# Output order by eight copies of token lists, and a third buffer for gathered rows, in a fused attention and expert kernel

## The chip, the cores and the metric

The kernel runs on one core of one Trainium2 chip. The metric is the device time of one execution in microseconds (us), the median of several runs. PE is TensorE, DVE is VectorE, ACT is ScalarE, POOL is GpSimd, and SP is SyncE, which issues most DMAs.

## What is computed

Attention with a band mask (4 batches, 8 heads, 576 positions, 64 per head) gives 2304 tokens of 512 numbers. Each token goes to one of 8 experts, and what comes out goes through a last layer with a cosine.

```python
def _moe_ref(x, expert_emb, tau, w1, w2):
    logits = xn @ en.T / tau            # xn, en: x and expert_emb at length 1
    expert_idx = np.argmax(logits, axis=1)
    probs = softmax(logits)
    gate_w = probs[np.arange(N), expert_idx]
    for e in range(E):
        mask = expert_idx == e
        h = np.maximum(x[mask] @ w1[e], 0.0)
        out[mask] = gate_w[mask, None] * (h @ w2[e])

def _moe2_ref(x, w_in, w_out):
    h = x @ w_in
    g = h * np.cos(h)
    return g @ w_out
```

## The kernel before

**Stage 1 (to about 147 us): attention and routing.** 18 tiles of 128 tokens. A tile's result goes to DRAM as rows of `x_d`. For each token the kernel finds the expert and the rank among that expert's tokens. `scatter` (L590) then writes each token's pair (token number, gate) by an indirect DMA into `tok_r`, which has a region of REG = 2688 pairs for each expert, zeroed at the start. So region e begins with the list of expert e's tokens, and zeros follow. `counts` (L701) makes `off`, the number of tokens before each expert, and its integer copy `meta`.

**Stage 2 (to about 435 us): the experts, one after another.** For expert e the job `list` loads 384 pairs of its region into `ix`, on SP (L854). For each of three blocks c of 128 tokens: `rows` gathers 128 rows of `x_d` into a tile `xr` by an indirect DMA on POOL (L859); `gate` multiplies them by the gates on DVE (L863); `turn` transposes them on PE (L868); `x hi` and `x lo` split them in two halves of 16 bits on ACT (L873) and DVE (L875), in the tile `xT`. The products follow: `mm` of even number (L1002) makes h, `relu` and `relu_lo` (L957, L961) split it, `mm` of odd number (L971) makes y. The third block has products of its own (`tail`, L979), which run only for an expert with more than 256 tokens. `emit_Y` (L944) puts y into `yT`, with expert e's columns from `off[e]` on, so `yT` holds the tokens sorted by expert. Beside this, expert weights are loaded (L241, 1 MB each, five buffers), measured (L250) and split (L273 on ACT, L275 on DVE), and the weights of the last layer are fetched (L766), rebuilt from 64-bit words (L772 to L784) and split (L806, L808).

**Stage 3: the last layer** in five blocks of columns of `yT` (u at L1186 and L1200, o at L1224). The rows that come out are in sorted order, so an indirect DMA writes each tile of 128 rows to its tokens' places in `out` (L1292), by the list `idx`.

**Where `idx` comes from.** `places` (L918) works out on DVE, in four operations, each token's place in the sorted order, `pu`. `place` (L928) then writes 128 token numbers to these places in `tok_d` by an indirect DMA on POOL, 18 times. `placed` (L936) loads `tok_d` into `idx` on SP.

**What sets the order.** In stage 2 the jobs are given to a planner (`Plan`, L77) with a queue, a cost and the jobs that they come after. It emits them by its own estimate of start times, and where several could start within a small time of each other it takes the one with the longest way to the end (`rank`). So every engine, and SP's queue of DMAs, has one fixed order, and a job that is not ready holds up what stands behind it. The buffers enter as jobs to come after: `rows` number k comes after `turn` number k - 2, for two `xr` buffers (L1040):

```python
plan.add(("rows", e, c), "POOL", 1.1, lambda e=e, c=c: x_do(e, c, "rows"), ("list", e), ("turn", (k - 2) // 3, (k - 2) % 3), ("rows", (k - 1) // 3, (k - 1) % 3))
```

Of the kernel before, what the change touches and what calls it, by code (L numbers as in the profile page):

```python
# [19 lines left out]
ALU = mybir.AluOpType  # L20
AX = mybir.AxisListType
ENG = mybir.EngineType
# [33 lines left out]
CUT = 4  # L56

BIAS1 = {'lo': -5, 'scale': -5, 'k': -5, 'v': 6, 'sent': -8, 'counts': -5, 'load': -10}
BIAS = {'u first': 15, 'csquare': 5, 'off': -3, 't lo': 22, 'g': 5, 'yb lo': -2, 'places': -5}
HOLD1 = 0.6  # L60
HOLD = 0.35
TAIL = 1.3
# [103 lines left out]
def tile_kernel(ctx, tc, qh, kh, vh, c16_h, c32_h, emb, tau, w1h, w2h, win_h, wout_h, out):  # L166
# [5 lines left out]
    x_d = dram.tile([NTOK, D], F32, name="x_d")  # L172

    tok_r = dram.tile([E * REG, 2], U32, name="tok_r")
    tok_d = dram.tile([NTOK, 1], U32, name="tok_d")

    c32 = const.tile([128, 256 + E + NT], F32, name="c32")
    ident, perm, iota, tokf = c32[:, 0:128], c32[:, 128:256], c32[:, 256:256 + E], c32[:, 256 + E:256 + E + NT]
# [12 lines left out]
    tri = const.tile([128, E, E], F32, name="tri")  # L191
    off = const.tile([128, E], F32, name="off")
    meta = const.tile([1, 2 * E + 1], I32, name="meta")

# [33 lines left out]
    with tc.manual_schedule():  # L228
        wst = ctx.enter_context(tc.tile_pool(name="wst", bufs=5, side="left"))
        with ExitStack() as p12:  # L230
            c12 = p12.enter_context(tc.tile_pool(name="c12", bufs=1, side="left"))
            zero = c12.tile([128, 512], U16, name="zero")
            wtp = p12.enter_context(tc.tile_pool(name="wtp", bufs=4, side="left"))
            wsm = p12.enter_context(tc.tile_pool(name="wsm", bufs=3, side="left"))
            stg, wt = {}, {}
# [70 lines left out]
            with ExitStack() as p1:  # L306
# [16 lines left out]
                head = lambda j: slice(64 * j, 64 * j + 64)  # L323
                blank = cst.tile([128, E * REG // 64], U32, name="blank")
                tau_b = cst.tile([128, 1], F32, name="tau_b")
                ent = cst.tile([128, 4, E], F32, name="ent")
                q_t = {}

# [428 lines left out]
            class Conv:  # L757
# [28 lines left out]
                def flat(self, g):  # L786
                    return self.pieces[g].rearrange("p a n -> p (a n)")
# [46 lines left out]
            with ExitStack() as p2:  # L834
# [20 lines left out]
                    return ix  # L855

                def x_rows(ix, c):
                    xr = hs.tile([128, D], F32, name="xr", tag="xr")
                    G.indirect_dma_start(out=xr, out_offset=None, in_=x_d, in_offset=bass.IndirectOffsetOnAxis(ap=ix[:, c, 0:1], axis=0))  # L859
                    return xr  # L860

# [36 lines left out]
                why = "numbers of tokens"  # L898
                zb = zero.bitcast(BF16)
                for t in (*h3, y3) + (y3,) * WARM2:  # L900
                    T.matmul(out=t.rearrange("p a b -> p (a b)"), lhsT=zb[:, 0:128], rhs=zb[:, 0:512], start=True, stop=True)
                nre = [nc.values_load(wide[0:1, e:e + 1], engines=[ENG.PE], min_val=0, max_val=len(TAILS), skip_runtime_bounds_check_because=why) for e in range(E)]
                T.matmul(out=y3.rearrange("p a b -> p (a b)"), lhsT=zb[:, 0:128], rhs=zb[:, 0:512], start=True, stop=True)
                offr = {}

                def offset(e, q):
                    engine = {"DVE": ENG.DVE, "ACT": ENG.Activation}[q]
                    offr[e, q] = nc.values_load(meta[0:1, e:e + 1], engines=[engine], min_val=0, max_val=NTOK, skip_runtime_bounds_check_because=why)

                pp = hs.tile([128, NT, E], F32, name="pp", tag="pp", bufs=1)
                df = hs.tile([128, E], F32, name="df", tag="df", bufs=1)
                ps_ = hs.tile([128, NT], F32, name="ps_", tag="ps_", bufs=1)
                pu = hs.tile([128, NT], U32, name="pu", tag="pu", bufs=1)
                toks = []

                def places(k):  # L918
                    if k == 0:
                        V.tensor_tensor(out=df, in0=base0, in1=off, op=ALU.subtract)  # L920
                    elif k == 1:
                        V.tensor_tensor(out=pp, in0=oh_all, in1=df.unsqueeze(1).to_broadcast([128, NT, E]), op=ALU.mult)
                    elif k == 2:
                        V.tensor_reduce(out=ps_, in_=pp, axis=AX.X, op=ALU.add)
                    else:
                        V.tensor_tensor(out=pu, in0=slot_all, in1=ps_, op=ALU.subtract)

                def place(t):  # L928
                    if t:
                        G.memset(half[:, 2:3], 0.5)  # L930
                    ins = G.indirect_dma_start(out=tok_d, out_offset=bass.IndirectOffsetOnAxis(ap=pu[:, t:t + 1], axis=0), in_=pay[:, t, 0:1], in_offset=None)
                    for o in toks:
                        tc.declare_no_dep(ins.ins, o.ins, reason="no two tokens have a place in common")
                    toks.append(ins)

                def placed():  # L936
                    ins = SP.dma_start(out=idx, in_=tok_d.rearrange("(c p) o -> p (c o)", p=128))
                    for o in toks:
                        tc.add_manual_dep(ins.ins, o.ins.name, mybir.DependencyInfo(mybir.DependencyClass.Sync, mybir.DependencyReason.DATA), reason="the places of all tokens")

                yps = {}

# [36 lines left out]
                def tail(m):  # L979
                    e = m // 2  # L980
                    def part(width):
                        for f in range(8):
                            if m % 2 == 0:
                                w = piece(m, f)
                                for n in range(12):
                                    c, (a, b) = n // 3, terms[n % 3]
                                    T.matmul(out=h3[f // 4][:, f % 4, 0:width], lhsT=w[:, a, 128 * c:128 * c + 128], rhs=xts[e][1][:, 4 * b + c, 0:width], start=n == 0, stop=n == 11)
                            else:
                                y_part(m, f, range(4), tail_h(width), tail_y(width), (0,), (3,))

                    if m % 2:
                        T.matmul(out=flat(y3), lhsT=zb[:, 0:128], rhs=zb[:, 0:512], start=True, stop=True)
                    with tc.If(nre[e] > 0):
                        part(TAILS[0])

# [40 lines left out]
                for e in range(E):  # L1036
                    plan.add(("list", e), "DMA", 0.5, lambda e=e: x_do(e, 0, "list"), ("sent", NT - 1), *[("gate", e - 2, c) for c in range(3)])
                    for c in range(3):
                        k = 3 * e + c
                        plan.add(("rows", e, c), "POOL", 1.1, lambda e=e, c=c: x_do(e, c, "rows"), ("list", e), ("turn", (k - 2) // 3, (k - 2) % 3), ("rows", (k - 1) // 3, (k - 1) % 3))  # L1040
                        plan.add(("row", e, c), "DMA", 1.0, lambda: None, ("rows", e, c))
                        plan.add(("gate", e, c), "DVE", 0.4, lambda e=e, c=c: x_do(e, c, "gate"), ("row", e, c), ("x scale", 4))
                        plan.add(("turn", e, c), "PE", 0.43, lambda e=e, c=c: x_do(e, c, "turn"), ("gate", e, c))
                        plan.add(("x hi", e, c), "ACT", 0.6, lambda e=e, c=c: x_do(e, c, "hi"), ("turn", e, c), ("mm", 2 * e - 4, 7), ("tail", 2 * e - 4))
                        plan.add(("x lo", e, c), "DVE", 0.68, lambda e=e, c=c: x_do(e, c, "lo"), ("x hi", e, c))
# [44 lines left out]
                def rest(e, n_e, i):  # L1090
# [10 lines left out]
                    for m in (2 * e, 2 * e + 1):  # L1101
                        for f in range(8):
                            w = wtp.tile([128, 2, 512], F16, name="wt", tag="wt")
                            src = hs.tile([128, 512], F32, name="ws", tag="xr")
# [251 lines left out]
```

## Time and profile before

| | us |
|---|---|
| median of 3 runs | 835.05 |
| the runs | 829.94 to 837.76 |
| the profiled execution | 827.02 |
| its span in the trace | 825.2 |
| busy in it: PE / DVE / ACT / POOL | 736.4 / 436.4 / 448.9 / 180.5 |

All times in the rows come from the one profiled execution and count from the start of its span; 1.8 us of its time lie outside the span. A timeline row has start, duration, engine, line, operation, tiles and count, and in brackets the idle time of the engine before it with what ended it. An idle time ended by "issue" is one for which the profile shows no semaphore.

### The profile page before, as it was taken

The numbers are of one execution on the slowest core, as the hardware profiler recorded it, in microseconds if no ns is written. First come the engines' busy times: TensorE is split into PE (matmuls) and PEld (weight loads), VectorE is DVE, ScalarE is ACT, GpSimd is POOL, SyncE is SP. The second block draws the span as 40 slices with busy tenths as digits, with TensorE's granted clock in tenths as the row PEclk, the third lists the DMA queues.
The fourth block names the chain that finished last, engine by engine and source line by source line (L and its number), as shares of the span: only waits on it lengthen the run. The fifth ranks groups of instructions, "written<-read, shape, count | busy, mean of one in ns | idle before, by whom it ended". The sixth has DMA issues, their size and how long they took to land. (4 is left out here: it accounts for less than half of the span.)

```text
span 825.2 us, 15933 instructions
## 1 busy us (share of the span) xinstructions
PE 736.4 (89%) x6537; PEld 484.2 (59%) x6537; DVE 436.4 (53%) x893; ACT 448.9 (54%) x705; POOL 180.5 (22%) x224
## 2 busy tenths in 40 slices
PE   6879889358999889969888989999999999999995
PEld 3657677246989768858873444444444445645642
DVE  5445536536786798867896981255015502521510
ACT  2434656272976889857566981276027602822810
POOL 0022223463020011000000530244114411421420
PEclk9998958598999989989999999999999999999998
DMA  8996930876656467543330000100000000000000
GB/s 269 297 282 194 294 146 15 257 116 146 207 202 238 154 208 255 176 170 116 116 106 29 0 1 1 51 1 2 26 26 1 1 26 26 0 14 26 1 14 26
DMA packets 27289, 87.39 MB, mean 106 GB/s; under 512 B 9528, under 2 KB 10040, under 8 KB 22080
## 3 DMA queue, kind: packets, MB, share of 16 engines
q1 hardware_dynamic: 19296, 68.06, 26.1%
q0 software_dynamic: 4512, 11.04, 4.4%
q10 hardware_dynamic: 3392, 7.08, 2.7%
q8 instruction: 59, 0.97, 0.5%
q14 instruction: 30, 0.25, 0.1%
HBM read 76.53 MB, written 9.64 MB: 104 GB/s over the span
## 5 line engine op out<-in xcount | busy, mean ns | idle before, releaser
L1186 PE MATMUL u<-yb,win 128*128 128x512 f16 (+1 forms) x924 | 179.8, 357 | 0.0
L1224 PE MATMUL o<-wst,g 128*128 128x512 f16 x672 | 145.7, 379 | 0.0
L1224 PEld LDWEIGHTS <-g 128*128 128x128 f16 x864 | 84.6, 98 | 104.0 <-issue 1.7
L1186 PEld LDWEIGHTS <-win 128*128 128x128 f16 x924 | 90.4, 98 | 88.8
L971 PE MATMUL y<-h,wt 128*128 128x256 f16 (+1 forms) x1152 | 109.7, 257 | 11.1 <-issue 10.1
L1220 POOL TENSOR_TENSOR g<-gg,g 128x512 f16<-128x512 f32 (+1 forms) x80 | 85.6, 1074 | 125.0 <-ACT g L1218 124.0
L971 PEld LDWEIGHTS <-wt 128*128 128x128 f16 x1152 | 97.2, 99 | 22.4 <-issue 12.5
L1002 PE MATMUL hps<-xT,wt 128*128 128x256 f16 x768 | 94.3, 284 | 17.7 <-DVE xT L875 10.6
L1002 PEld LDWEIGHTS <-wt 128*128 128x128 f16 x768 | 78.0, 102 | 31.6 <-issue 17.6
L1215 DVE SCALAR_TENSOR_TENSOR gg<-u,q 128x512 f32<-128x512 f32 (+1 forms) x80 | 50.6, 637 | 74.3 <-ACT q L1212 74.1
L1207 ACT ACTIVATE kk<-u,quart,ku 128x512 int32<-128x512 f32 (+1 forms) x80 | 58.2, 733 | 51.7 <-PE u L1186 51.5
L275 DVE SCALAR_TENSOR_TENSOR wt<-wst,wsc,wt 128x1024 f16<-128x1024 f32 x64 | 79.4, 1279 | 3.1 <-ACT wt L273 3.0
L273 ACT ACTIVATE wt<-wst,wsc 128x1024 f16<-128x1024 f32 x64 | 69.0, 1143 | 15.3 <-DVE wsc L217 7.8
L1210 DVE SCALAR_TENSOR_TENSOR q<-u,ku,kk 128x512 f32<-128x512 f32 (+1 forms) x80 | 54.8, 689 | 32.0 <-ACT kk L1207 32.0
L859 POOL DMA_INDIRECT xr<-x_d,ix x24 | 26.6, 1107 | 202.1 <-PE hps L868 101.4
L250 ACT ACTIVATE junk<-wst 128x2048 bf16<-128x2048 f32 x32 | 61.0, 1905 | 10.5 <-DMA wst<-in_w1h 10.4
L1286 ACT ACTIVATE osb<-o,ku 128x512 f32<-128x512 f32 x6 | 4.1, 687 | 97.3 <-PE o L1224 97.3
L1212 ACT ACTIVATE q<-q,quart 128x512 f32<-128x512 f32 (+1 forms) x80 | 53.1, 669 | 5.3 <-DVE q L1210 5.0
L1288 DVE TENSOR_SCALAR osb<-o,ku 128x512 f32<-128x512 f32 x8 | 6.0, 750 | 92.4 <-PE o L1224 92.4
L1292 POOL DMA_INDIRECT out<-osb,idx x18 | 17.5, 975 | 147.8 <-DVE osb L1288 92.0
L1218 ACT ACTIVATE g<-gg 128x512 f16<-128x512 f32 (+1 forms) x80 | 45.8, 575 | 1.4 <-DVE gg L1215 1.4
L1224 PE MATMUL u<-wst,g 128*128 128x512 f16 x192 | 41.8, 379 | 2.3 <-ACT wst L806 1.6
(194 smaller groups left out, 864.9 us busy)
## 6 DMA issues: line engine op xcount, KB each, us to landing
wst<-in_w1h SPq DMA_DIRECT2D x16, 1024.0 KB
wst<-in_w2h SPq DMA_DIRECT2D x16, 1024.0 KB
vb<-in_vh SPq DMA_DIRECT2D x8, 1040.0 KB
raw<-in_winh SPq DMA_DIRECT2D x16, 512.0 KB
raw<-in_wouth SPq DMA_DIRECT2D x16, 512.0 KB
x_d<-x ACTq DMA_DIRECT2D x18, 256.0 KB
q<-in_qh SPq DMA_DIRECT2D x8, 512.0 KB
kr<-in_kh ACTq DMA_DIRECT2D x8, 256.0 KB
```

Source lines behind the costliest of these rows:

```text
L250: S.activation(out=junk[:, 0:k], in_=src, func=ACTF.Square, accum_out=wmx[m][:, i:i + 1])
L273: S.activation(out=hi, in_=src, func=ACTF.Copy, scale=wsc[:, m, 0:1])
L275: V.scalar_tensor_tensor(out=lo, in0=src, scalar=wsc[:, m, 0:1], in1=hi, op0=ALU.mult, op1=ALU.subtract)
L971: T.matmul(out=dst(d), lhsT=w[:, a, 128 * d:128 * d + 128], rhs=src(f, b), start=f == 0 and k == 0 and d in firsts, stop=f == 7 and k == 2 ...
L1002: T.matmul(out=hps[e, f // 2][:, f % 2], lhsT=w[:, a, 128 * c:128 * c + 128], rhs=xts[e][0][:, 4 * b + c, :], start=n == 0, stop=n == 11)
L1186: T.matmul(out=us[f], lhsT=win[f][:, a, 128 * c:128 * c + 128], rhs=ybs[b][:, a2, c, :], start=k == 0, stop=k == 11)
L1207: S.activation(out=ks[f], in_=us[f], func=ACTF.Identity, scale=ku[:, 0:1], bias=quart[:, 0:1])
L1210: V.scalar_tensor_tensor(out=qs[f], in0=us[f], scalar=ku[:, 0:1], in1=ks[f], op0=ALU.mult, op1=ALU.subtract)
L1212: S.activation(out=qs[f], in_=qs[f], func=ACTF.Sin, scale=PI2, bias=quart[:, 1:2])
L1215: V.scalar_tensor_tensor(out=gs[f], in0=us[f], scalar=SH, in1=qs[f], op0=ALU.mult, op1=ALU.mult)
L1220: G.tensor_tensor(out=g_t[f][:, 1], in0=gs[f], in1=g_t[f][:, 0], op=ALU.subtract)
L1224: T.matmul(out=o, lhsT=g_t[f][:, a, 128 * t:128 * t + 128], rhs=wout[f][:, a2, :], start=f == 0 and k == 0, stop=f == 15 and k == 2)
```

## The change

`places` and the 18 indirect writes go. In their place, for each expert in turn, POOL loads `off[e]` into a register and issues one plain DMA from DRAM to DRAM. It copies the first 2304 pairs of expert e's region of `tok_r` to `tok_d`, from place `off[e]` on, as 16 rows of 144 pairs. Each copy overwrites what the one before it left behind its own tokens, so copy e waits for copy e - 1. Copy e is also put behind the last gather of expert e + 1. `tok_d` becomes twice as long and two words wide. `placed` loads the first word of its first 2304 pairs, behind the last copy.

The gathered rows `xr` get three buffers, and `rows` number k comes after `turn` number k - 3. To make room, `zero` shrinks from 512 to 128 columns (the matmuls that blank a PSUM bank then read it four times), and `tri` moves to a pool that ends with stage 1.

```diff
-    tok_d = dram.tile([NTOK, 1], U32, name="tok_d")
+    tok_d = dram.tile([2 * NTOK, 2], U32, name="tok_d")
...
-            zero = c12.tile([128, 512], U16, name="zero")
+            zero = c12.tile([128, 128], U16, name="zero")
...
-                    xr = hs.tile([128, D], F32, name="xr", tag="xr")
+                    xr = hs.tile([128, D], F32, name="xr", tag="xr", bufs=3)
...
+                def blank_3(t):
+                    T.matmul(out=t, lhsT=zb, rhs=zb.unsqueeze(1).to_broadcast([128, 4, 128]), start=True, stop=True)
...
-                def place(t):
-                    if t:
-                        G.memset(half[:, 2:3], 0.5)
-                    ins = G.indirect_dma_start(out=tok_d, out_offset=bass.IndirectOffsetOnAxis(ap=pu[:, t:t + 1], axis=0), in_=pay[:, t, 0:1], in_offset=None)
...
+                def place(e):
+                    to = tok_d[bass.ds(offr[e, "POOL"], NTOK)]
+                    scattered(G.dma_start(out=to.rearrange("(a b) w -> a (b w)", a=16), in_=tok_r[e * REG:e * REG + NTOK].rearrange("(a b) w -> a (b w)", a=16)))

                 def placed():
-                    ins = SP.dma_start(out=idx, in_=tok_d.rearrange("(c p) o -> p (c o)", p=128))
...
+                    SP.dma_start(out=idx, in_=tok_d[0:NTOK, 0:1].rearrange("(c p) o -> p (c o)", p=128))
...
-                        plan.add(("rows", e, c), "POOL", 1.1, lambda e=e, c=c: x_do(e, c, "rows"), ("list", e), ("turn", (k - 2) // 3, (k - 2) % 3), ("rows", (k - 1) // 3, (k - 1) % 3))
+                        plan.add(("rows", e, c), "POOL", 1.1, lambda e=e, c=c: x_do(e, c, "rows"), ("list", e), ("turn", (k - 3) // 3, (k - 3) % 3), ("rows", (k - 1) // 3, (k - 1) % 3))
...
-                for k in range(4):
-                    plan.add(("places", k), "DVE", 0.2, lambda k=k: places(k), ("places", k - 1))
-                for t in range(NT):
-                    plan.add(("place", t), "POOL", 1.1, lambda t=t: place(t), ("places", 3), ("place", t - 1))
-                plan.add("placed", "DMA", 1.0, placed, ("place", NT - 1))
+                for e in range(E):
+                    plan.add(("off", e, "POOL"), "POOL", 0.45, lambda e=e: offset(e, "POOL"), ("list", e), ("place", e - 1))
+                    plan.add(("place", e), "POOL", 1.1, lambda e=e: place(e), ("off", e, "POOL"), ("copied", e - 1), ("rows", min(e + 1, E - 1), 2))
+                    plan.add(("copied", e), "DMA", 0.5, lambda: None, ("place", e))
+                plan.add("placed", "DMA", 1.0, placed, ("copied", E - 1))
```

The planner's entry that delayed `places` (`'places': -5` in `BIAS`) goes too.

## Rows read from the trace of the kernel before

**Rows 1.** Stretches by stage: us, busy time (count) of each engine, PE clock, DMA share, GB/s

```profile
147.80:200.60 52.80, 30.00 (x222) 24.32 (x223) 25.37 (x46) 21.43 (x29) 28.44 (x42) 0.74 0.70 153
200.60:434.70 234.10, 209.83 (x2217) 187.71 (x2216) 181.81 (x312) 178.20 (x244) 18.46 (x17) 0.97 0.53 182
434.70:825.20 390.50, 377.54 (x1837) 180.22 (x1837) 148.39 (x237) 178.13 (x295) 105.71 (x116) 0.99 0.04 14
```

**Rows 2.** Timeline of PE around expert 0's second product (L971)

```profile
159.19 1.12 PE L868 MATMUL hps<-c,xr 128*128 128x128 f32 x4 [0.92 <-DVE xr L863]
...
176.09 2.23 PE L971 MATMUL y<-h,wt 128*128 128x256 f16 x19
188.38 10.37 PE L971 MATMUL y<-h,wt 128*128 128x256 f16 x77 [10.05 <-issue]
198.59 0.60 PE L868 MATMUL hps<-c,xr 128*128 128x128 f32 x4
...
200.60 5.40 PE L1002 MATMUL hps<-xT,wt 128*128 128x256 f16 x48
```

**Rows 3.** DMA queues: packets, MB, share of 16 engines

```profile
q8 instruction: 59, 0.97, 0.5%
```

**Rows 4.** Stretches of 2 us, columns as in rows 1

```profile
150.00:152.00 2.00, 0.00 (x0) 0.00 (x0) 1.30 (x5) 1.73 (x1) 1.43 (x2) 0.50 1.03 418
...
182.00:184.00 2.00, 0.00 (x0) 0.00 (x0) 0.00 (x0) 2.00 (x3) 0.09 (x1) 0.50 0.88 72
...
194.00:196.00 2.00, 2.00 (x21) 1.80 (x19) 1.97 (x4) 0.10 (x1) 0.00 (x0) 1.00 0.06 8
...
200.00:202.00 2.00, 1.85 (x19) 1.64 (x17) 1.90 (x7) 0.00 (x0) 1.43 (x2) 1.00 0.97 397
```

**Rows 5.** Waits from 138 to 212 us: total us, times, longest us

```profile
DVE xr L863 <- DMA xr<-x_d,ix: 16.6, 5, 8.5
...
POOL tok_d L931 <- DMA tok_d<-pay,pu: 7.1, 3, 4.3
```

**Rows 6.** POOL's groups, whole span: busy us, mean ns, idle before and its releasers

```profile
L859 POOL DMA_INDIRECT xr<-x_d,ix x24 | 26.6, 1107 | 202.1 <-PE hps L868 101.4 <-DMA raw<-in_winh 26.5 <-DVE wsc L217 23.5
L931 POOL DMA_INDIRECT tok_d<-pay,pu x18 | 18.3, 1018 | 10.0 <-DMA tok_d<-pay,pu 7.1 <-issue 2.5 <-DVE pu L926 0.4
...
L930 POOL MEMSET half<- 128x1 f32 x17 | 2.1, 125 | 0.0
```

**Rows 7.** Timeline of DVE in the same stretch

```profile
179.94 1.29 DVE L961 SCALAR_TENSOR_TENSOR h<-h,h 128x512 f16<-128x512 f32 x2 [1.47 <-issue]
189.75 0.55 DVE L863 TENSOR_SCALAR xr<-xr,ix,xsc 128x512 f32<-128x512 f32 x1 [8.52 <-DMA xr<-x_d,ix]
190.21 4.87 DVE L275 SCALAR_TENSOR_TENSOR wt<-wst,wsc,wt 128x1024 f16<-128x1024 f32 x4
...
199.85 0.69 DVE L875 TENSOR_TENSOR xT<-hps,xT 128x512 f16<-128x512 f32 x1
```

**Rows 8.** Timeline of SP's DMA issues, and of ACT at the load

```profile
192.71 0.33 SPq L241 DMA_DIRECT2D wst<-in_w1h  x1
...
202.73 1.91 ACT L250 ACTIVATE junk<-wst 128x2048 bf16<-128x2048 f32 x1 [2.91 <-DMA wst<-in_w1h]
...
205.60 3.79 SPq L766 DMA_DIRECT2D raw<-in_winh  x1
```

**Rows 9.** Waits from 205 to 440 us, PE and DVE

```profile
PE hps L1002 <- DVE xT L875: 10.1, 7, 3.6
...
DVE xr L863 <- DMA xr<-x_d,ix: 5.7, 2, 3.5
PE hps L1002 <- ACT xT L873: 4.8, 1, 4.8
```

**Rows 10.** PE's waits from 440 to 520 us

```profile
PE u L1224 <- ACT wst L806: 1.6, 1, 1.6
```

**Rows 11.** Register loads of `off`: duration ns min/median/max, first and last start

```profile
L908 DVEq TENSOR_LOAD <-meta x8: 300/306/552, 169.3 to 428.8; - x8
```

**Rows 12.** POOL's timeline: the gather for expert 1's second block

```profile
175.87 0.98 POOL L859 DMA_INDIRECT xr<-x_d,ix  x1 [0.79 <-DMA tok_d<-pay,pu]
```

More of the change, by code (lines that the diff above doesn't have):

```diff
@@ L58 @@
 BIAS1 = {'lo': -5, 'scale': -5, 'k': -5, 'v': 6, 'sent': -8, 'counts': -5, 'load': -10}
-BIAS = {'u first': 15, 'csquare': 5, 'off': -3, 't lo': 22, 'g': 5, 'yb lo': -2, 'places': -5}
+BIAS = {'u first': 15, 'csquare': 5, 'off': -3, 't lo': 22, 'g': 5, 'yb lo': -2}
 HOLD1 = 0.6
@@ L190, in tile_kernel @@
     cnt = const.tile([128, E], F32, name="cnt")
-    tri = const.tile([128, E, E], F32, name="tri")
     off = const.tile([128, E], F32, name="off")
@@ L325, in tile_kernel @@
                 tau_b = cst.tile([128, 1], F32, name="tau_b")
+                tri = cst.tile([128, E, E], F32, name="tri")
                 ent = cst.tile([128, 4, E], F32, name="ent")
@@ L899, in tile_kernel @@
                 zb = zero.bitcast(BF16)
+                def blank_3(t):
+                    T.matmul(out=t, lhsT=zb, rhs=zb.unsqueeze(1).to_broadcast([128, 4, 128]), start=True, stop=True)
                 for t in (*h3, y3) + (y3,) * WARM2:
-                    T.matmul(out=t.rearrange("p a b -> p (a b)"), lhsT=zb[:, 0:128], rhs=zb[:, 0:512], start=True, stop=True)
+                    blank_3(t)
                 nre = [nc.values_load(wide[0:1, e:e + 1], engines=[ENG.PE], min_val=0, max_val=len(TAILS), skip_runtime_bounds_check_because=why) for e in range(E)]
-                T.matmul(out=y3.rearrange("p a b -> p (a b)"), lhsT=zb[:, 0:128], rhs=zb[:, 0:512], start=True, stop=True)
+                blank_3(y3)
@@ L904, in tile_kernel @@
                 offr = {}
                 def offset(e, q):
-                    engine = {"DVE": ENG.DVE, "ACT": ENG.Activation}[q]
+                    engine = {"DVE": ENG.DVE, "ACT": ENG.Activation, "POOL": ENG.Pool}[q]
                     offr[e, q] = nc.values_load(meta[0:1, e:e + 1], engines=[engine], min_val=0, max_val=NTOK, skip_runtime_bounds_check_because=why)
-                pp = hs.tile([128, NT, E], F32, name="pp", tag="pp", bufs=1)
-                df = hs.tile([128, E], F32, name="df", tag="df", bufs=1)
@@ L914, in tile_kernel @@
[L914 to L926, printed above, removed]
@@ L928, in place @@
-                def place(t):
-                    if t:
-                        G.memset(half[:, 2:3], 0.5)
-                    ins = G.indirect_dma_start(out=tok_d, out_offset=bass.IndirectOffsetOnAxis(ap=pu[:, t:t + 1], axis=0), in_=pay[:, t, 0:1], in_offset=None)
-                    for o in toks:
-                        tc.declare_no_dep(ins.ins, o.ins, reason="no two tokens have a place in common")
-                    toks.append(ins)
+                def place(e):
+                    to = tok_d[bass.ds(offr[e, "POOL"], NTOK)]
+                    scattered(G.dma_start(out=to.rearrange("(a b) w -> a (b w)", a=16), in_=tok_r[e * REG:e * REG + NTOK].rearrange("(a b) w -> a (b w)", a=16)))
@@ L936, in placed @@
                 def placed():
-                    ins = SP.dma_start(out=idx, in_=tok_d.rearrange("(c p) o -> p (c o)", p=128))
-                    for o in toks:
-                        tc.add_manual_dep(ins.ins, o.ins.name, mybir.DependencyInfo(mybir.DependencyClass.Sync, mybir.DependencyReason.DATA), reason="the places of all tokens")
+                    SP.dma_start(out=idx, in_=tok_d[0:NTOK, 0:1].rearrange("(c p) o -> p (c o)", p=128))
                 yps = {}
@@ L991, in tail @@
                     if m % 2:
-                        T.matmul(out=flat(y3), lhsT=zb[:, 0:128], rhs=zb[:, 0:512], start=True, stop=True)
+                        blank_3(y3)
                     with tc.If(nre[e] > 0):
@@ L1103, in rest @@
                             w = wtp.tile([128, 2, 512], F16, name="wt", tag="wt")
-                            src = hs.tile([128, 512], F32, name="ws", tag="xr")
+                            src = hs.tile([128, 512], F32, name="ws", tag="xr", bufs=3)
                             SP.dma_start(out=src, in_=(w1h if m % 2 == 0 else w2h)[e, f // 4, :, 512 * (f % 4):512 * (f % 4) + 512])
```

## Prediction

> **What bounds the kernel now.** I read the table of stretches first. Its columns give each engine's busy time, so the idle time of TensorE (PE) by stage can be taken from it [rows 1]. After 434.7 us (the last layer) PE is busy for 377.5 of 390.5 us: nothing of the change lies there, and it can only start earlier. From 200.6 to 434.7 us (experts 1 to 7) PE is busy for 209.8 of 234.1 us. But from 147.8 to 200.6 us (expert 0) it is busy for only 30.0 of 52.8 us, at a mean granted clock of 0.74 of full speed. That is the stage in which the 18 indirect writes stand, so I read it next, engine by engine.
>
> PE's timeline there [rows 2]: the second product of expert 0 starts at 176.09, stops after 19 of its 96 matmuls, starts again at 188.38 after 10.05 us of idle time, and ends at 198.6; expert 1 starts at 200.60. The idle time is labelled "issue": no semaphore ended it. What PE can lack without a semaphore is its own instructions, and these come over the DMA engines too, in 59 packets [rows 3]. So I looked at the DMA engines in the same stretch, in windows of 2 us [rows 4]. From 150 to 152 us, as the first indirect write is issued, they move 418 GB/s at a share of 1.03. From 182 to 184 us the share is 0.88, but only 72 GB/s come through: the engines are occupied and deliver a fifth. From 194 to 196 us a 1 MB weight load issued at 192.71 is pending, and 8 GB/s move; ScalarE gets that load only at 202.73 [rows 8]. At 200 to 202 us the rate is back at 397 GB/s. The list of waits names the same stretch: POOL waits 7.1 us for the landing of indirect writes to `tok_d`, up to 4.3 at once, and VectorE (DVE) waits 16.6 us for gathered rows, up to 8.5 at once [rows 5]. My reading is that the 18 indirect writes (2304 single words of 4 bytes to one small DRAM tensor) clog the DMA engines, and that this and not POOL's time is their price.
>
> **The change part by part.**
>
> *POOL's time.* The writes take 18.3 us busy, their memsets 2.1, and 10.0 us of idle time stand in front of them [rows 6]: 30 us of POOL. Direct worth on the path: one gather starts 0.79 us late behind them [rows 12]. I take 0; bounds 0 and -0.8.
>
> *The four `places` operations.* They fall into a stage in which DVE is busy for 25.4 of 52.8 us [rows 1], while PE waits for gathered rows. 0; bounds 0 and -1.
>
> *The DMA stall.* If it goes, PE runs its remaining 77 matmuls straight on. At the rate of 0.108 us each (48 matmuls of the same size in 5.40 us, less the modelled end of the last, [rows 2]) the 77 take 8.3 us, so they end at 178.3 + 8.3 = 186.6 in place of 198.6. Of these 12.0 us, 10 are the idle time and 2 the half clock after it (the 77 took 10.37 us). Expert 1 also needs DVE. Its work between 189.75 and 199.85 us is one unbroken run: a gate held 8.52 us by gathered rows, four conversions of weights (4.87 us), other conversions, and then the low half of `xT` at 199.85 [rows 7]. It could start at 181.24, when the operation before it ends. If its order stays, expert 1 starts 8.5 us earlier; if the third buffer lets the gates go ahead, by the full 12.0.  I take -11, nearer to the larger end, since the third buffer does bring the gate forward: bounds -8.5 and -12.
>
> *The third buffer.* The gather for expert 1's second block starts at 175.87 us [rows 12], since buffer and queue were not free; with three it needs only the turn of expert 0's second block, which begins at 159.19 [rows 2]. That is counted above. Later it brings little: DVE waits only 5.7 us for gathered rows after 205 us, while PE's waits for `xT` (10.1 + 4.8 us) end with conversions on DVE and ScalarE, not with gathers [rows 9]. 0; bounds 0 and -7.5 (half of these waits, if the planner now puts turns earlier).
>
> *The eight copies.* Each adds a register load (0.3 us on DVE, for want of one on POOL [rows 11]) and an issue, 1.1 us if it is like POOL's gather [rows 6]: 8 x 1.4 = 11 us of POOL, in a stage where it is busy for 18.5 of 234.1 us [rows 1] and where gathers wait 101 us for buffers anyway [rows 6]. Behind a waiting copy stands the gather of a later expert, and DVE waits for that; a copy waits for the one before it, issued an expert (some 33 us) earlier, or, for the last two, one transfer earlier. 0; bounds 0 and +11 if every microsecond showed. What they do to the DMA engines no row shows; the nearest are the indirect writes themselves, and the third rival below has that price.
>
> *The load of `idx`.* It moves from 198 us to behind the last copy, after the last gather can start: some 380 us, among the fetches of `wout` on SP. At present the fetch behind it keeps SP for 3.79 us [rows 8]. The conversions of `wout` are late for PE at 483 us, by 1.6 us [rows 10]. I take 0; bounds 0 and +3.8.
>
> *The blanking matmuls* keep 512 columns, and the moved tensors issue nothing: 0. *The planner* makes its order anew behind the counts. All idle time of PE after 200.6 us is 24.3 us [rows 1]; a new order can give or take some of it. I take 0, with 5 us to either side as an estimate: half of the 10.1 us of PE's largest group of waits there [rows 9].
>
> **Sum.** -11 us. The profiled execution took 827.0 us (span 825.2), so 816 in its place; the median of the runs is 835.05, 8.0 above, so 824.
>
> One rule of the Trainium skill bears on the copies: in "DMA: Bandwidth & Descriptors", section "Specifications", transfers under 512 bytes are done as read-modify-write. By it the words of 4 bytes would be the trouble, and the copies' runs of 1152 bytes (144 entries of 8 bytes) would not, which leaves the sum at -11; no row here separates the size of a write from their number.
>
> **Rivals.**
>
> 1. *The gain is there, and part of it is lost later.* The last layer's conversions run on DVE and ScalarE, busy for 181.8 and 178.2 of 234.1 us [rows 1], and the late `idx` load holds `wout` back. Price: 3.8 us for the load, and 1.6 for a second wait like that at 483 us: -11 + 5.4 = -5.6, 829 us. For it: the wait at 483 exists already. Against it: DVE and ScalarE have over 50 us of idle time in that stage.
>
> 2. *The stall is not the writes'.* PE ran out of instructions by itself, or weights, gathers and fetches together are too much. Then only POOL's 0.8 us and the DVE operations go: -1, 834 us. For it: the label names no releaser. Against it: after 205 us the same loads and gathers run, and no "issue" wait is among PE's there (its two largest groups are in [rows 9]).
>
> 3. *The copies clog the DMA engines too.* They also write DRAM from POOL's queue, and they now stand inside the stage in which PE is bound. The price is that of an indirect write's landing, 7.1 us in 3 waits, 2.4 us each [rows 5]; for 8 copies 19 us: -11 + 19 = +8, 843 us. It decides from 11 / 8 = 1.4 us of PE time per copy. For it: nothing in the profile says that number and size of the words made the stall. Against it: a copy has 16 rows where 2304 words were written, and gathers lie ahead of their use.
> The Trainium skill speaks for this one: by "DMA: Bandwidth & Descriptors", section "Queues, rings and completion order", the write that reports a transfer lands only after every earlier write of that DMA engine, in all its queues, so copies to DRAM can hold back weights and gathers on the same engines. The late weight load agrees with it, without proving it.
>
> 4. *More than the stall.* The third buffer also ends half of PE's waits for `xT`: -11 - 7.5, 817 us.
>
> **Chances and range.** Forecast (824 us, its own range 821 to 828) 0.50; rival 1, 0.18; rival 2, 0.12; rival 3, 0.12; rival 4, 0.08. About 1% (8.4 us) is what a measurement of this kernel can tell from no change; the three runs of before lie 7.8 us apart. Faster by over 1% means under 826.7: most of the forecast (0.43), rival 4 and a little of rival 1 make 0.53. Slower by over 1% is rival 3 and a badly made order, 0.13. The rest is 0.34. The range leaves out the far half of rival 4 below and half of rival 3 above: 815 to 838.
>
> **What would show it.** Right: in expert 0's second product no idle time over 1 us, expert 1 starting at 187 to 193 us, no window with a pending load under 100 GB/s, DVE's wait for gathered rows in that stage at half or less, and every later stage shifted by as much. Copies that land without a dip in GB/s show the fifth step right. Wrong: if the 10 us at 178 remain (rival 2), if PE has new waits of 2 us or more behind each copy (rival 3), or if expert 1 starts earlier and the last layer does not (rival 1).

## The result, and the profile after

The changed kernel takes 823.8 us (median of 16 runs, 818.49 to 830.34), the kernel before 834.06 us in the same comparison (16 runs, 829.94 to 838.27): a ratio of 0.9876, with a 95% interval of 0.9848 to 0.9904. So it is faster by 1.2%, and 824.0 us had been predicted. The number hides an early gain that is a little larger than the sum had it and a late loss that the sum did not have; this section shows both. The profiled execution of after took 821.14 us (span 819.5). The one of before, with its 827.0 us, lies below all 16 runs of that comparison, so the two profiles are only 5.9 us apart, and I compare stages rather than spans.

The table of stretches of after, for the stages of [rows 1] (expert 0; experts 1 to 7; the last layer), in the same columns:

```profile
146.40:186.60 40.20, 27.70 (x222) 23.64 (x222) 22.58 (x39) 22.36 (x29) 9.53 (x9) 0.83 0.63 230
186.60:426.60 240.00, 212.10 (x2217) 188.94 (x2216) 181.99 (x313) 176.66 (x243) 20.77 (x23) 0.94 0.52 172
426.60:819.50 392.90, 380.00 (x1837) 181.01 (x1837) 149.63 (x239) 179.45 (x297) 106.48 (x116) 0.98 0.04 14
```

Expert 0's stretch is 12.6 us shorter than in [rows 1] (40.2 against 52.8), near the 11 of the prediction. But the next one, in which PE does the same work, is 5.9 us longer, and the last layer 2.4 us longer. The 5.9 us were not predicted; the 2.4 us are about what before differs from itself there (390.4 and 392.5 us in the table below).

PE's timeline around expert 0's second product, now line 953 (compare [rows 2]):

```profile
155.92 1.12 PE L868 MATMUL hps<-c,xr 128*128 128x128 f32 x4 [9.50 <-DVE xr L863]
...
172.81 10.64 PE L953 MATMUL y<-h,wt 128*128 128x256 f16 x96
183.29 1.04 PE L868 MATMUL hps<-c,xr 128*128 128x128 f32 x8
...
186.63 10.64 PE L984 MATMUL hps<-xT,wt 128*128 128x256 f16 x96 [0.21 <-DVE xT L875]
```

All 96 matmuls run in one piece; the 10.05 us of "issue" and the half clock behind it are gone, and expert 1 starts at 186.63 in place of 200.60. The stretches of 2 us just before show a weight load issued at 179.73 flowing at once, where [rows 4] had 72 and 8 GB/s:

```profile
180.00:182.00 2.00, 2.00 (x21) 1.79 (x20) 2.00 (x2) 2.00 (x3) 0.00 (x0) 1.00 0.57 152
182.00:184.00 2.00, 2.00 (x21) 1.87 (x19) 1.28 (x4) 1.39 (x5) 0.00 (x0) 1.00 1.03 418
```

PE's instructions still come in 59 packets, 0.97 MB in all, as in [rows 3]; only what stood in their way is gone. DVE's wait for gathered rows from 138 to 212 us fell from 16.6 to 8.7 us [rows 5]:

```profile
DVE xr L863 <- DMA xr<-x_d,ix: 8.7, 3, 6.2
```

POOL's groups (compare [rows 6]), then SP's late load of `idx`. A copy costs POOL half of a gather, and the load keeps SP for 0.43 us, not 3.79:

```profile
L859 POOL DMA_INDIRECT xr<-x_d,ix x24 | 26.1, 1087 | 178.5 <-PE hps L868 108.7 <-DVE wsc L216 34.6 <-DVE win L782 21.1
...
L918 POOL DMA_DIRECT2D tok_d<-tok_r x8 | 4.4, 546 | 4.0 <-DVE wt L274 4.0
```

```profile
362.56 0.43 SPq L921 DMA_DIRECT2D idx<-tok_d  x1
```

To find where the 13 us at expert 1 went, I read PE's timeline at five marks, in every kernel of this study: the first transposition of gathered rows (L868, "first turn"), the first matmul of expert 1 and of expert 5 (L1002 of before, L984 of after), the first matmul of the last layer (L1192, L1174), and the end; the other kernels have the same instructions on lines of their own. All in us:

| kernel | order, form, buffers | to first turn | to expert 1 | to expert 5 | to last layer | to the end |
|---|---|---|---|---|---|---|
| before | old, writes, 2 | 157.2 | 43.4 | 125.6 | 108.6 | 390.4 |
| e4, before again | old, writes, 2 | 161.0 | 45.0 | 129.3 | 108.5 | 392.5 |
| after | new, copies, 3 | 155.9 | 30.7 | 123.1 | 116.9 | 392.9 |
| e10, after again | new, copies, 3 | 152.6 | 31.9 | 121.8 | 118.0 | 393.3 |
| e3 | new, none, 3 | 156.7 | 31.8 | 121.8 | 118.5 | 392.5 |
| e1 | new, copies, 2 | 161.7 | 32.8 | 126.3 | 118.6 | 390.2 |
| e2 | new, writes, 3 | 157.1 | 43.9 | 123.4 | 116.5 | 394.9 |
| e5 | old, copies, 2 | 149.8 | 33.4 | 127.3 | 108.9 | 391.6 |
| e6 | old, copies, 3 | 146.4 | 33.5 | 128.5 | 108.1 | 392.4 |
| e11, e6 again | old, copies, 3 | 151.1 | 32.8 | 126.5 | 108.6 | 391.8 |
| e7 | old, writes 256 B apart, 2 | 155.8 | 33.3 | 126.9 | 108.7 | 392.4 |
| e9 | old, writes 64 B apart, 2 | 157.1 | 33.4 | 127.0 | 108.7 | 392.6 |
| e12 | old, writes 16 B apart, 2 | 159.0 | 37.1 | 125.1 | 108.9 | 392.4 |
| e8 | old, writes of 512-byte rows, 2 | 150.8 | 33.2 | 129.8 | 108.7 | 392.4 |

Read before and after by columns: the stall gives 13 us, experts 1 to 4 give 2.5 to 7.5, and experts 5 to 7 take 8 to 10 back. In the column "to last layer" the kernels fall into two groups without overlap, 108.1 to 108.9 and 116.5 to 118.6, and what divides them is whether the planner's order is the old one or a new one. The profiles confirm the column "order": from just ahead of the first turn to the last layer, DVE runs the same 349 operations in the same sequence in before and in every kernel marked old (the four of `places`, which only some have, left out). "New" is not one order, though. After and e10 share one, e2 and e3 have it but for a few operations, and e1 has another.

What the new order costs there, read from the stretch of experts 5 to 7, after first and then before:

```profile
309.70:426.60 116.90, 96.25 (x997) 84.72 (x996) 88.35 (x150) 77.00 (x109) 4.54 (x6) 0.89 0.44 141
```

```profile
326.20:434.80 108.60, 92.95 (x1002) 83.16 (x1003) 84.39 (x147) 74.68 (x105) 5.45 (x6) 0.97 0.41 136
```

Of the 8.3 us, 5.0 are idle time of PE (20.65 against 15.65) and 3.3 are longer matmuls, at a mean granted clock of 0.89 against 0.97 (in e10 22.1 us of idle time and 0.89 again). Where PE stands idle in after: two of its groups of waits from 186 to 432 us, then rows of its timeline.

```profile
PE o L1174 <- DVEq L1114: 7.9, 1, 7.9
...
PE hps L984 <- DVE xT L875: 5.6, 4, 5.0
```

```profile
351.85 5.28 PE L984 MATMUL hps<-xT,wt 128*128 128x256 f16 x24 [5.00 <-DVE xT L875]
362.77 3.57 PE L984 MATMUL hps<-xT,wt 128*128 128x256 f16 x16 [5.64 <-DVE h L943]
```

Behind each wait the matmuls take 0.22 us each, twice the 0.11 of the 96 above: the granted clock is 0.50 (1.2 GHz) from 351.9 to 357.1 us and from 362.8 us to at least 366.3, where the row ends with the window that was read, each time after PE stood idle. DVE's timeline names what stood in front of `xT` and `h`:

```profile
346.33 4.87 DVE L274 SCALAR_TENSOR_TENSOR wt<-wst,wsc,wt 128x1024 f16<-128x1024 f32 x4
351.12 0.68 DVE L875 TENSOR_TENSOR xT<-hps,xT 128x512 f16<-128x512 f32 x1
...
360.24 0.43 DVE L780 TENSOR_SCALAR wst<-ab 128x512 uint32<-128x512 uint32 x1 [1.28 <-ACT ab L772]
...
362.03 0.69 DVE L943 SCALAR_TENSOR_TENSOR h<-hps,h 128x512 f16<-128x512 f32 x1
```

Four conversions of weights, and later nine operations on `wout` of which one waits for ACT, are queued ahead of what PE needs next. That these are the loss is read from the trace; no run moves them alone. The wait at the barrier ahead of the last layer (7.9 us above) was shorter in the kernel before:

```profile
PE o L1192 <- DVEq L1132: 4.5, 1, 4.5
```

### The profile page after: what moved, and what is told of

The parts are those of the page before. It is cut to its first block, busy times and chain, and to the rows that moved or that the text cites. A ratio compares the mean times of both kernels' runs of the same rounds, so it can differ in the third digit from the quotient of the medians.

```text
span 819.5 us, 15896 instructions
## 1 busy us (share of the span) xinstructions
PE 737.5 (90%) x6537; PEld 483.6 (59%) x6537; DVE 434.9 (53%) x889; ACT 449.8 (55%) x705; POOL 163.6 (20%) x197
## 5 line engine op out<-in xcount | busy, mean ns | idle before, releaser
L953 PE MATMUL y<-h,wt 128*128 128x256 f16 (+1 forms) x1152 | 108.1, 255 | 1.2 <-DVE h L943 0.4
L984 PE MATMUL hps<-xT,wt 128*128 128x256 f16 x768 | 94.7, 290 | 12.7 <-DVE h L943 7.1
L984 PEld LDWEIGHTS <-wt 128*128 128x128 f16 x768 | 80.2, 105 | 26.4 <-issue 13.4
L1192 DVE SCALAR_TENSOR_TENSOR q<-u,ku,kk 128x512 f32<-128x512 f32 (+1 forms) x80 | 54.8, 690 | 32.4 <-ACT kk L1189 32.3
L859 POOL DMA_INDIRECT xr<-x_d,ix x24 | 26.1, 1087 | 178.5 <-PE hps L868 108.7
```

The source lines that it names most:

```text
L953: T.matmul(out=dst(d), lhsT=w[:, a, 128 * d:128 * d + 128], rhs=src(f, b), start=f == 0 and k == 0 and d in firsts, stop=f == 7 and k == 2 ...
L984: T.matmul(out=hps[e, f // 2][:, f % 2], lhsT=w[:, a, 128 * c:128 * c + 128], rhs=xts[e][0][:, 4 * b + c, :], start=n == 0, stop=n == 11)
L1192: V.scalar_tensor_tensor(out=qs[f], in0=us[f], scalar=ku[:, 0:1], in1=ks[f], op0=ALU.mult, op1=ALU.subtract)
```

## The experiments

Each expectation stands as it was written ahead of the run. Ratios are to the kernel before on the same chip.

**Copies, two buffers** (the third buffer undone):

```diff
-name="xr", tag="xr", bufs=3)
+name="xr", tag="xr")
...
-... ("turn", (k - 3) // 3, (k - 3) % 3) ...
+... ("turn", (k - 2) // 3, (k - 2) % 3) ...
```

> The changed kernel with two xr buffers again and rows k after turn k - 2: the eight copies alone. Theory A (the 18 indirect writes clog the DMA engines; removing them is the gain): expert 0's second product runs without an idle time over 1 us, and the median is 822 to 828 us, a ratio to before of 0.985 to 0.993. Rival B (the third buffer, which lets gathers go early, is the gain): 831 to 835 us, ratio 0.996 to 1.002, and VectorE waits 5 us or more for gathered rows in expert 0.

Measured: 833.21 us, ratio 0.9974 (0.9939 to 1.0009). Theory A had the stall right and the time wrong, and the time of rival B came for another reason. Expert 1 starts early (32.8 us after the first turn), so the copies end the stall without the third buffer. But the late loss is as large as in after (118.6 us), and experts 1 to 4 take 126.3 us, not 122 to 123. These 3 to 5 us stand between two kernels that differ in the buffer and in the order that the planner made for it, so they belong to both together.

**Writes, three buffers** (the other half of the change; small tiles of `places` stand in PSUM to make room):

```diff
-                    xr = hs.tile([128, D], F32, name="xr", tag="xr")
+                    xr = hs.tile([128, D], F32, name="xr", tag="xr", bufs=3)
-... ("turn", (k - 2) // 3, (k - 2) % 3) ...
+... ("turn", (k - 3) // 3, (k - 3) % 3) ...
```

> The kernel before with three xr buffers and rows k after turn k - 3, the 18 indirect writes kept: the buffer alone. To make room, the three small tiles of the places calculation stand in PSUM. Theory A: the idle time of some 10 us in expert 0's second product stays, the median is 830 to 836 us, ratio 0.995 to 1.003. Rival B: it goes, 822 to 828 us, ratio 0.985 to 0.993.

Measured: 836.77 us, ratio 0.9985 (0.9948 to 1.0023), as theory A had it but for 0.8 us in the median. The stall is there (43.9 us), and the late loss too (116.5). PE's idle time stands elsewhere, in the same place of the work:

```profile
185.88 12.62 PE L975 MATMUL y<-h,wt 128*128 128x256 f16 x96 [5.89 <-PEq L997]
```

PEq is PE's sequencer, which reaches line 997 late. So neither half alone moves the time beyond its interval, and the late loss comes with either half; with each the planner orders the work anew.

**No work for the order of the output** (after, without copies and `idx` load):

```diff
-                    plan.add(("place", e), "POOL", 1.1, lambda e=e: place(e), ...)
-                plan.add("placed", "DMA", 1.0, placed, ("copied", E - 1))
-... ap=idx[:, c:c + 1] ...
+... ap=pay[:, c, 0:1] ...
```

> The changed kernel without copies and without the load of idx; the rows go out by the token numbers in their natural order, so the sorting back of the output rows is left out, and the time is the floor of all order work. Theory A with copies that cost nothing: within 2 us of the changed kernel (822 to 826 us). Rival C (copies and the late load of idx take back part of the gain in experts 6 and 7): 816 to 820 us.

Measured: 823.9 us, ratio 0.9867 (0.982 to 0.9914), after's own time to 0.1 us. The interval is some 4 us wide to either side; from the first turn to the end the profiles are closer, 664.6 us against 663.6 and 665.0. So the eight copies and the late load cost nothing that can be measured, and the late loss (118.5 us here) is not theirs.

**Before again.** 

> The kernel before, unchanged, for a second profile of it. Theory A: an idle time of 8 to 12 us in expert 0's second product, windows under 100 GB/s while a weight load is pending; ratio 1.00. Rival D (the idle time was an accident of one execution): under 3 us of it.

Measured: 838.41 us beside 834.68, a ratio of 1.0043 (1.0003 to 1.0083) of a kernel to itself, so an interval that misses 1 by so little decides nothing. Expert 1 starts at 45.0 us, and the late stage takes 108.5. In expert 0's second product there are not the 8 to 12 us of idle time that theory A named, nor under 3, as rival D had it:

```profile
188.11 11.46 PE L971 MATMUL y<-h,wt 128*128 128x256 f16 x77 [4.47 <-issue]
```

The stall repeats in size; how its idle time is split does not.

**Copies in the old order.** The planner's old jobs are kept and issue nothing, so that the order stays as it was; POOL issues each copy behind the last gather of the next expert.

```diff
-                    plan.add(("place", t), "POOL", 1.1, lambda t=t: place(t), ("places", 3), ("place", t - 1))
+                    plan.add(("place", t), "POOL", 1.1, lambda: None, ("places", 3), ("place", t - 1))
...
+                        if c == 2 and e:
+                            place(e - 1)
+                            if e == E - 1:
+                                place(e)
```

> The kernel before in its own order on PE, VectorE and ScalarE (the planner still sees the old jobs, which issue nothing), with two xr buffers; in place of the 18 indirect writes, POOL issues copy e right behind the last gather of expert e + 1, and idx is loaded behind all jobs of the planner. Theory E (the indirect writes cost some 12 us in expert 0, and the new order that the planner makes gives 8 to 10 us of that back in experts 5 to 7): expert 1 starts 31 to 34 us after the first turn of a block, experts 5 to 7 take as long as in the kernel before (107 to 110 us), and the median is 820 to 826 us, ratio 0.982 to 0.990. Rival F (the late loss has another cause, such as the earlier start itself): experts 5 to 7 take 115 us or more, and the ratio is 0.994 to 1.000.

> The same with three xr buffers in the old order. Theory E: 1 to 3 us faster than the run with two, 818 to 824 us, ratio 0.979 to 0.988, and faster than the changed kernel. Rival F: like the changed kernel or slower, 0.986 to 0.994.

Measured: 815.32 us with two buffers, ratio 0.9814 (0.9765 to 0.9863), and 812.95 us with three, 0.9797 (0.9748 to 0.9847). Both medians are 5 us under what theory E named, as that of the kernel before is in this comparison (829.6 us); the ratios fit to 0.001. Rival F is out: the late stage is back at 108 to 109 us with the same copies, and with the early start, so the loss is the order's. The third buffer does nothing clear in this order. The stretch of experts 5 to 7 in the kernel with three:

```profile
308.50:416.50 108.00, 92.36 (x1001) 82.92 (x1002) 84.48 (x147) 74.56 (x105) 6.16 (x8) 0.96 0.43 134
```

**Words 256 bytes apart.** The kernel before, with the same 18 writes of the same 2304 words, but each in a place of its own:

```diff
-    tok_d = dram.tile([NTOK, 1], U32, name="tok_d")
+    tok_d = dram.tile([64 * NTOK, 1], U32, name="tok_d")
...
-V.tensor_tensor(out=pu, in0=slot_all, in1=ps_, op=ALU.subtract)
+V.tensor_tensor(out=ps_, in0=slot_all, in1=ps_, op=ALU.subtract)
+V.tensor_scalar(out=pu, in0=ps_, scalar1=64.0, scalar2=None, op0=ALU.mult)
...
```

> The kernel before with the 2304 words of tok_d 256 bytes apart, written by the same 18 indirect writes (one more VectorE operation of 0.15 us). If many words in one small stretch of DRAM hold the DMA engines up: the idle time in expert 0's second product falls below 3 us, expert 1 starts 31 to 36 us after the first turn. If each single word does: as before, 43 to 45 us after it.

**Rows of 512 bytes.** The same 18 writes, each of 128 rows of 512 bytes (rows of ones, so this kernel leaves the sorting back out):

```diff
-    tok_d = dram.tile([NTOK, 1], U32, name="tok_d")
+    tok_d = dram.tile([NTOK, 128], F32, name="tok_d")
...
-... in_=pay[:, t, 0:1], in_offset=None)
+... in_=ones_f, in_offset=None)
...
```

> The kernel before, where each of the 18 indirect writes puts 128 rows of 512 bytes of ones into a tensor of 2304 rows, at the same places in the same order; the rows go out by the token numbers in natural order, so the sorting back is left out. If the size of 4 bytes is the trouble: expert 1 starts 31 to 36 us after the first turn. If the number of rows or POOL's path is: 43 us or more after it.

Measured: 818.41 us, ratio 0.9855 (0.9778 to 0.9931), for the words apart, and 816.42 us, 0.9831 (0.9755 to 0.9906), for the rows, from two runs each; expert 1 starts at 33.3 and 33.2 us. So neither the number of writes, nor POOL's time, nor the 4 bytes by themselves are the trouble: 18 writes of 4-byte words from the same queue stall nothing if the words are not neighbours, and rows of 512 bytes side by side stall nothing either. In the kernel with words apart, PE's second product and a stretch in which POOL issues writes (1.81 us busy) while a weight load runs at 233 GB/s:

```profile
174.04 10.64 PE L972 MATMUL y<-h,wt 128*128 128x256 f16 x96
```

```profile
182.00:184.00 2.00, 2.00 (x21) 1.79 (x19) 2.00 (x4) 0.71 (x2) 1.81 (x3) 1.00 0.78 233
```

**Words and pairs 64 bytes apart.** As the one with 256, and `tok_r` too, which stage 1 writes in the same way:

```diff
-    tok_r = dram.tile([E * REG, 2], U32, name="tok_r")
-    tok_d = dram.tile([NTOK, 1], U32, name="tok_d")
+    tok_r = dram.tile([8 * E * REG, 2], U32, name="tok_r")
+    tok_d = dram.tile([16 * NTOK, 1], U32, name="tok_d")
...
```

> The kernel before with its 18 indirect writes to tok_d and its order, but each word of tok_d stands 64 bytes from the next (256 in the run before), and the pairs of tok_r, which stage 1 writes with 18 indirect writes too, also stand 64 bytes apart. Theory (small words that are neighbours in DRAM are what is slow): the words land in about 3 us as at 256 bytes apart, expert 1 starts 33 to 34 us after the first turn, and the writes of tok_r, whose median is 6.1 us from issue to landing in the run with words 256 bytes apart, also land in about 3 us, so that the first gather of stage 2 starts some 3 us earlier after the last write of tok_r (6.7 us after it in the changed kernel). Rival A (64 bytes are not far enough): expert 1 starts 43 to 45 us after the first turn as before, and tok_r lands in 6 us. Rival B (tok_r's landing has another cause, such as the number of its DMA queues or the wait for the data): tok_d is well and tok_r stays at 6 us.

Measured: 810.98 us, ratio 0.9789 (0.9722 to 0.9856). Its profiled execution is the longest of its four, with PE's clock at 0.50 from 110 to 130 us, ahead of the stages read here. The DMA issues (the last column is the median in us from issue to landing), first of the kernel with 256 bytes, where `tok_r` is as in before, then of this one:

```profile
tok_r<-pay,slot_u POOLq DMA_INDIRECT x18, 6.2
tok_d<-pay,pu POOLq DMA_INDIRECT x18, 2.8
```

```profile
tok_r<-pay,slot_u POOLq DMA_INDIRECT x18, 3.0
tok_d<-pay,pu POOLq DMA_INDIRECT x18, 2.9
```

Both rivals fall: 64 bytes are enough, and the pairs of `tok_r` land in half the time once they are apart (side by side their median is 6.1 or 6.2 us in four profiles, 4.5 in e10 and 5.1 in e11). The last part of the expectation missed: the first gather starts 6.0 us after the last write of `tok_r` (148.19 - 142.14), 0.6 us earlier than in after and not 3, since the list's own load stands in between.

**Words 16 bytes apart.** As the one with 256, with 4 in place of 64:

```diff
+    tok_d = dram.tile([4 * NTOK, 1], U32, name="tok_d")
...
+V.tensor_scalar(out=pu, in0=ps_, scalar1=4.0, scalar2=None, op0=ALU.mult)
...
```

> The kernel before with its 18 indirect writes to tok_d and its order, each word of tok_d 16 bytes from the next (4 in the kernel before, 64 and 256 in the two runs with words apart). Theory A (what is slow is several words in one piece of 64 bytes): four words still share one, so part of the stall is left: expert 1 starts between 34 and 45 us after the first turn, and the words take more than 4 us to land. Theory B (only words next to each other, or within 16 bytes, get in each other's way): as at 64 bytes, expert 1 33 to 34 us after the first turn, the words land in about 3 us, and POOL waits for none of them.

Measured: 824.21 us, ratio 0.9877 (0.9713 to 1.0041, from two runs, so the mark says more than the time); expert 1 at 37.1 us, between 33.4 (64 bytes) and 43.4 (4 bytes). The profile has no landing times for this run. PE's instructions come late in small gaps again:

```profile
187.96 1.24 PE L972 MATMUL y<-h,wt 128*128 128x256 f16 x8 [0.31 <-issue]
189.44 0.27 PE L972 MATMUL y<-h,wt 128*128 128x256 f16 x1 [0.24 <-issue]
190.19 0.27 PE L972 MATMUL y<-h,wt 128*128 128x256 f16 x1 [0.47 <-issue]
```

This fits theory A: part of the stall is left while four words share 64 bytes. One profile at each distance shows a graded effect, not where its edge is. Words further apart also lie in a larger piece of DRAM, and no run separates the two.

The records of single DMA packets in the traces show the clog itself. In the 45 us behind the first turn, 59 packets take over 2 us in before, 68 in e4 and 59 in e2, the longest 8.1 us. With words 16 bytes apart there are 7, the longest 2.5 us, and in the ten other profiles of the table there is none. The slow packets are not those of the words: nearly all are 4 or 8 KB, on the queue of SP's loads and on POOL's, which gathers rows. Two of them in e4 (3.1 and 7.3 us), one in e2 and one in e12 are instructions, 16 KB each, which take about 1 us at the median. In before none is, so that its 10.05 us were a wait for instructions stays argued.

**After and the old order with three buffers, once more, on one chip.**

> The changed kernel once more, beside the next one on the same chip. In the profiles so far the time up to the first turn of expert 0 differs between 146 and 162 us although the code of that stage is the same in all of them; in that stage the granted clock of PE between 110 and 130 us is 0.50 in the kernel before, 0.75 here and 1.0 in the kernel with old order, copies and three buffers. Theory (which of these clocks a kernel gets is its own, and repeats): first turn at about 156 us again, median 822 to 826. Rival (it is by chance, execution by execution): first turn anywhere between 146 and 162.

> The kernel with the planner's old order, the copies and three buffers once more. Theory (repeats): first turn at 146 to 148 us with a clock near 1.0 between 110 and 130 us, median 811 to 816, some 10 us under the changed kernel of the same call, and all of that difference stands before the first turn (from the first turn to the end both take 662 to 664 us). Rival (chance): first turn as far off as 156 us, and the median with it, so that the two kernels cannot be told apart.

Measured: 819.65 us, ratio 0.9894 (0.9837 to 0.9952), and 813.61 us, 0.9837 (0.9774 to 0.99). The rival of chance was right: the first turn came at 152.6 and 151.1 us, where 155.9 and 146.4 had been. PE's clock in stage 1 differs as well; from 110 to 130 us, for the old order with three buffers, first the earlier run and then this one:

```profile
110.00:130.00 20.00, 17.45 (x237) 14.34 (x231) 13.99 (x84) 15.40 (x30) 9.77 (x17) 1.00 0.16 55
```

```profile
110.00:130.00 20.00, 18.97 (x188) 16.44 (x188) 11.50 (x71) 13.97 (x26) 6.62 (x12) 0.71 0.15 54
```

The same code has 1.00 in one execution and 0.71 in the next, and before has 0.50 in both of its profiles. Over the 14 profiles the clock goes with the first turn at its ends (0.96 to 1.00 with 146.4 to 150.8 us, 0.50 with 157.1 to 161.0), but not between them: e10 has 0.64 and 152.6 us, after 0.74 and 155.9. So differences of a few us in the column "to first turn" cannot be put down to the change. From the first turn to the end after takes 663.6 and 665.0 us, the old order with three buffers 662.5 and 659.8, before 668.0 and 675.3, so some of the difference does stand behind it. The old order's lead over after in medians (6 us on this chip) has overlapping intervals and stays open; the intervals of both lie below 1.

## Why the prediction was right

**The DMA stall: right in place and cause, a little small.** Taken at -11 with the larger bound at -12; measured 30.7 and 31.9 us from first turn to expert 1 in place of 43.4 and 45.0, so about -13. In the old order with two buffers, where DVE's order stays, it is 33.4 (e5), so -10 to -12: the term for the writes alone was well sized, and the rest came with the new order and its third buffer.
The reason was right only in part. "2304 single words of 4 bytes to one small DRAM tensor" clog the engines as small words that are neighbours; small or many alone is not enough, since 64 or 256 bytes apart the same words stall nothing. Nor are the engines always busy in the stall, as "clog" suggests: at 194 us their share was 0.06 with a load pending [rows 4].
The words 256 bytes apart land in 2.8 us, and expert 1 starts at 33.3 us, so size by itself is not what decides here. The rule of the Trainium skill that the prediction cited ("DMA: Bandwidth & Descriptors", section "Specifications", read-modify-write under 512 bytes) goes by size alone and would treat the words apart like the words side by side; the measurement decides. Whether reading and writing back is what makes neighbours slow, no run here shows.

**POOL's time, the four `places` operations, the eight copies, the load of `idx`: right at 0.** The kernel without copies and load takes 823.9 us against 823.8. Two prices behind the bounds were far off: a copy is issued in 0.55 us, not 1.1, and the load keeps SP for 0.43 us, not 3.8.

**The third buffer: 0 is right for the buffer alone.** Taken at 0 beyond the stall. In the old order, where nothing else changes, it does nothing clear. With the order that the planner makes for three buffers, experts 1 to 4 take 123.1, 121.8, 121.8 and 123.4 us; with e1's order and two, 126.3. So 3 to 5 us may be rival 4's mechanism at about half of its price, but no run separates buffer and order there.

**The planner: the step that failed.** "I take 0, with 5 us to either side" was the term for a new order, and 0 was too low. It measures +8 to +10 us in experts 5 to 7: PE's idle time grows by 5.0 us, and 3.3 us more go in matmuls at a lower clock behind the waits, a cost that the estimate from PE's waits alone [rows 9] left out. Against it stand 2.5 to 7.5 us won in experts 1 to 4. Net, from the first turn to the end, the new order with three buffers (663.6 and 665.0 us) is some 3 us behind the old order with copies (659.8 to 662.5), which is within the 5 us; e1's order with two buffers (668.0) is some 7 us behind e5 (661.2), which is not. That the sum came so near is luck in part: after gains 7.4 us in the stages that the change touches (the mean of two profiles each, 671.7 and 664.3), and the medians differ by 10.3 us in one comparison and by 6.3 (825.95 and 819.65) in the other, stage 1's chance clock included.

**The rivals.** Rival 1 had the form right (an early gain, partly given back), but neither of its reasons: the `idx` load costs nothing, and the wait at the last layer's conversions grew only from 1.6 us [rows 10] to 2.4. Rival 2 is false, since new addresses for the writes, with one more DVE operation, end the stall. Rival 3 is false at its first step: there is no 1.4 us per copy, nor any cost that the kernel without copies could show.
The Trainium skill's sentence behind rival 3 ("DMA: Bandwidth & Descriptors", section "Queues, rings and completion order") may hold; no run here shows a copy holding back a load.

**What would show it.** The idle time in expert 0's second product is gone, as asked; expert 1 at 186.63 us is just under the 187 to 193 that were named; DVE's wait for gathered rows is at 52%, where half or less was asked; "every later stage shifted by as much" is false, and that line of the list is the one that showed the failed step.

## What to carry to other kernels

When a stage has idle time that no semaphore ended, look at the DMA engines: few GB/s while a load is pending mean that something holds them up, whether their share is near 1 (72 GB/s at 0.88) or near 0 (8 GB/s at 0.06), and instructions come over them too. Before scattered writes are replaced, try their targets 64 bytes apart or more; here that took one more DVE operation and gave about what the rewritten kernel gives or more (0.9855 from two runs and 0.9789 from four, against 0.9876). A change to a planned kernel is two changes, what it does and the order that the planner makes of it: keep the old order with empty jobs once, to see the two apart, and compare from a mark behind any stage whose clock differs by chance.

## What the runs showed that was not expected

- Neighbouring 4-byte writes to DRAM delay weight loads, gathers and instructions on the DMA engines: expert 1 starts at 43.4 and 45.0 us with words 4 bytes apart, 37.1 at 16, 33.4 at 64 and 33.3 at 256, with the same number of writes and bytes. Pairs of 8 bytes show it as well, landing in 4.5 to 6.2 us side by side and in 3.0 us at 64 bytes apart. Ahead of the first turn, no DMA packet takes over 2 us in the kernel with pairs apart; in the other 13 profiles 3 to 29 do.
- The granted clock of stage 1 from 110 to 130 us ranges from 0.50 to 1.00 over the executions, and the first turn comes at 146.4 to 161.7 us, for work that the change hardly touches. What sets it is open: in the 10 us ahead, PE was busy for 7.3 us in before (then 0.50) and for 7.0 us in the old order with two buffers (then 0.96).
